# Attention operands laid out by the host: no transposes of q and k on the chip

## The chip, the cores and the metric

The kernel runs on one core of a Trainium2 chip. The metric is the device time of one execution in microseconds; lower is better. Three runs of the kernel before gave a median of 639.01 us (638.66 to 640.62).

## The reference

Three computations follow one another. All are float32 except the weights of the last, which arrive as 64-bit words.

```python
# attention, batch 2, 8 heads, 576 positions, head size 64
scores = q @ k.T / 8, masked; heads 0-3: 0 <= i-j < 32; heads 4-7: 0 <= i-j < 128 and (i-j) % 4 == 0
attn = softmax(scores);  x = (attn @ v), tokens 1152 x 512
# mixture: 4 experts, every token goes through all of them
out = sum_e p[:, e] * (relu(x @ w1[e]) @ w2[e])      # 512 -> 1024 -> 512
# last block
h = out @ w_in;  g = h * sigmoid(1.702 h);  result = g @ w_out   # 512 -> 2048 -> 512
```

## The kernel before

**Three stages.** Attention and the first expert are woven into each other and take about the first 156 us; then come the other three experts (line 799 on for the first product, 903 to 905 for the second), then the last block. Every large product is made of three products of rounded operands: high by high, low by high, high by low (`wh`, `wl`, `xh`, `xl`).

**Attention.** Heads are taken in pairs. Pairs 0 and 1 are "plain" (window 32), pairs 2 and 3 "dilated" (stride 4). The sequence of each batch is cut into a big and a small piece, so there are 16 parts, numbered 0 to 15 in the order of line 497: four big parts of batch 0 (pairs 2, 3, 0, 1), eight small ones, four big ones of batch 1. A big part has two groups, a small one has one; groups are numbered 0 to 23. A dilated part works by residue r of the position modulo 4, since a position sees only its own residue.

**Steps of a part or group.** `L` loads q and k of a part with tokens on partitions (`load_qk`, lines 213 and 217): rows of one position, 256 bytes a run for plain pairs and 1 KB for dilated ones. `T` transposes q or k on PE into PSUM (line 267; four transposes, two for a small plain part). `t` copies the transposed block to SBUF (line 270 on; `a` on ACT, `v` on DVE). `K` loads v (lines 232, 239, 243). `S` makes the scores of one group, or of two at once with their products alternating (line 324). `Q` masks them and takes the row minimum on DVE (line 332). `A` is the exponential with its row sum on ACT (line 337). `N` normalizes, on POOL (`p`) or DVE (`v`) (lines 358 to 360). `U` transposes the probabilities on PE (line 368), `c` copies them to SBUF, `V` multiplies by v (line 394), `C` and `R` store the result as high and low part `xh`, `xl`.

**The order** is written out by hand in `SCRIPT` (lines 22 to 58). Each word is emitted in that order, and every engine works through its own share of the words in that order; there is no other scheduler. Fillers from the first expert stand in the list: `W` loads a weight tile (line 144), `H` and `O` split it into high and low on ACT and on POOL or DVE (lines 159, 167), `G` and `F` are pieces of its first product (line 524), `2` of its second (lines 558 to 560), `h` and `l` the steps between. `P n` issues n "spin" products on constants (line 443). All loads are issued by SP from one queue, in list order.

**Dilated groups before.** `T` puts residues 0 and 2 of a head on partitions 0 to 63 and residues 1 and 3 on 64 to 127. Group x of a big dilated part takes the two residues of parity x for both heads (lines 294 to 301); its four score products all read one half of the partitions. In a small part the two halves are used in turn within each tile.

**Weights.** `w_load` (line 135) cuts a 128-row weight tile out of the full matrix. For the last block `w64_tasks` (line 703) loads 64-bit words in pieces of 512 KB, converts them and stores them to DRAM for later.

Of the kernel before, what the change touches and what calls it, by code (L numbers as in the profile page):

```python
# [27 lines left out]
G 0 1 h, R 3, N 6 v, T 5 k, T 5 q, U 6, L 7, W 1 1, K 3, c 5 v, O 0 0 p 0, t 4 k a, Q 7, A 7, c 6 a, H 1 0 0,
t 5 k a, t 4 q v, L 8, K 4, K 5, L 9, N 7 p, t 5 q v, V 5, C 5 v, S 8, G 0 1 l, S 9, T 6 q, U 7, T 7 k, F 0 7 8,
H 1 0 1, Q 8, R 5, O 1 0 v 2, L 10, W 2 0, K 6, D, A 8, K 7, O 1 0 p 1, N 8 p, G 0 2 h, G 1 1 l, T 6 k, T 7 q, U 8,  # L30
c 7 a, Q 9, t 6 q v, A 9, t 6 k v, K 8, W 3 0, L 11, t 7 q a, H 0 1 0, t 7 k a, c 8 v, N 9 v, V 7, S 10, F 1 0 1,
G 1 1 h, T 8 k, F 0 6 7, T 8 q, F 0 0 1, U 9, F 0 2 3, Q 10, C 7 a, A 10, H 0 1 1, R 7, O 1 0 v 0, F 0 3 6, F 1 6 7,
F 0 1 2, N 10 v, H 1 1 0, h 0, t 8 q v, c 9 v, O 0 1 v 0, t 8 k a, V 8, S 11, C 8 v, S 12, F 1 7 8, V 9, F 1 3 4,
F 1 2 3, T 9 q, Q 11, Q 12, A 12, A 11, l 0, O 0 1 v 1, F 1 5 6, R 8, F 1 4 5, O 1 0 p 3, F 2 1 6, T 10 q, U 10,
N 12 v, 2 0 0, F 2 0 1, F 1 1 2, O 0 1 v 2, c 10 a, K 9, L 12, L 13, K 10, N 11 p, U 11, T 9 k, t 9 q v, t 10 q v,
H 1 1 1, h 1, t 9 k a, C 9 a, F 2 6 8, c 11 v, O 0 1 v 3, T 10 k, U 12, t 10 k a, V 10, V 11, h 2, R 9, l 1, S 13,
c 12 v, H 2 0 0, S 14, C 11 a, V 12, l 2, R 11, O 2 0 p 0, Q 13, Q 14, H 3 0 0, C 12 a, T 11 q, 2 0 1, F 3 7 8,
2 1 0, 2 0 2, F 3 6 7, T 11 k, F 3 5 6, F 3 1 2, F 3 2 5, 2 0 3, F 3 0 1, 2 1 1, H 2 0 1, A 14, C 10 a, t 11 q v,
R 12, O 1 1 p 1, O 1 1 v 0, O 2 0 p 1, O 2 0 p 2, A 13, K 11, W 3 1, W 2 1, L 14, K 12, N 14 v, O 1 1 p 2, O 2 0 p 3,
R 10, h 3, t 11 k a, N 13 v, l 3, U 14, U 13, c 14 a, c 13 v, H 3 0 1, F 4 2 8, 2 1 2, 2 1 3, F 4 0 1, F 4 1 2, S 15,  # L40
V 14, h 4, V 13, C 14 a, H 3 1 0, H 2 1 0, H 2 1 1, R 14, C 13 v, R 13, O 3 0 p 1, O 1 1 v 3, O 3 0 p 2, O 2 1 p 2,
O 2 1 p 3, Q 15, 2 2 0, H 3 1 1, B 15 v, X 15, Y 15, F 5 0 2, 2 2 1, 2 3 0, F 5 2 5, F 5 5 8, 2 3 1, 2 2 2, T 12 k,
2 3 2, 2 2 3, O 3 0 p 3, l 4, N 15 v, t 12 k a, h 5, K 13, O 2 1 v 1, l 5, O 3 1 p 2, O 3 0 p 0, L 15, U 15, F 6 4 6,
F 6 2 4, F 6 6 8, 2 3 3, T 12 q, F 6 0 2, w, t 12 q v, c 15 a, V 15, h 6, S 16 17, l 6, Q 17, Q 16, C 15 a, B 16 v,
# [8 lines left out]
F 12 5 6, 2 9 3, F 12 3 4, c 20 v, t 15 k v, c 21 v, S 22, Q 22, S 23, Q 23, V 21, F 12 4 5, A 23, B 22 p, X 22,
h 12, Y 22, l 12, F 13 0 8, F 14 1 2, F 14 2 4, F 14 0 1, C 21 a, R 21, 2 11 0, N 23 v, N 22 v, h 13, 2 10 1, U 22,
2 10 2, 2 11 1, 2 10 3, 2 11 2, F 14 4 5, F 14 5 7, F 15 5 6, 2 11 3, F 14 7 8, 2 12 0, F 15 4 5, F 15 6 8, l 13,
c 22 v, F 15 3 4, U 23, h 14, 2 13 0, c 23 a, V 23, 2 12 1, C 23 v, 2 12 2, 2 12 3, 2 13 1, F 15 0 3, 2 13 2, h 15,
l 14, R 23, 2 13 3, l 15
# [4 lines left out]
def fused_kernel(ctx: ExitStack, tc: tile.TileContext, q, k, v, dp, w1, w2, w_in, w_out, out):  # L62
# [18 lines left out]
    B, H, S, D = q.shape  # L81
    NT, DM = out.shape
    E, _, FF1 = w1.shape
    FF2 = w_in.shape[1]
# [3 lines left out]
    NPAIR = H // 2  # L88
    J = S // 4
# [45 lines left out]
    def w_load(s, which):  # L135
        e, fp = divmod(s, F1 // 2)
        fs = slice(fp * 2 * P, (fp + 1) * 2 * P)
        if which == 0:
            t = stg.tile([P, KT, 2 * P], F32, tag="stg", name=f"st1_{s}")
            src = w1[e][:, fs].rearrange("(k p) f -> p k f", p=P) if e < E else late[s - 4 * E, 0]  # L140
        else:
            t = stg.tile([P, 2, DM], F32, tag="stg", name=f"st2_{s}")
            src = w2[e][fs, :].rearrange("(t p) d -> p t d", p=P) if e < E else late[s - 4 * E, 1]
        nc.sync.dma_start(out=t, in_=src)
        wst[s, which] = t
# [45 lines left out]
    raw = {}  # L191
# [15 lines left out]
    def load_qk(b, pr, kind):
        j0, j1 = t_part(b, pr, kind)
        for nm, src in (("q", q), ("k", k)):
            if plain(pr):  # L210
                t = ap_.tile([96, (j1 - j0) // 24, 2, D], F32, tag="raw", bufs=8, name=f"raw{nm}{b}{pr}{kind}")
                for h in range(2):
                    nc.sync.dma_start(out=t[:, :, h, :], in_=src[b, 2 * pr + h, 4 * j0:4 * j1, :].rearrange(
                        "(i s) d -> s i d", s=96))
            else:
                t = ap_.tile([j1 - j0, 2, 4, D], F32, tag="raw", bufs=8, name=f"raw{nm}{b}{pr}{kind}")
                nc.sync.dma_start(
                    out=t, in_=src[b, 2 * pr:2 * pr + 2, 4 * j0:4 * j1, :].rearrange("h (j r) d -> j h r d", r=4))
            raw[nm, b, pr, kind] = t

    def blocks_of(b, kind):
        j0, j1 = PARTS[b, kind]
        return range(j0 // 16, j1 // 16)

    def load_v(b, pr, kind):

        if plain(pr):
            bl = blocks_of(b, kind)
            t = ap_.tile([96, 6, 2, D], F32, tag="v", bufs=6, name=f"v{b}{pr}{kind}")
            i0 = bl[0]  # L230
            if i0 == 0:
                nc.sync.dma_start(out=t[:, 0, :, :], in_=v[b, 2 * pr:2 * pr + 2, 0:96, :].rearrange("h s d -> s h d"))
                i0 = 1
            n = bl[-1] + 1 - i0
            for h in range(2):
                head = v[b, 2 * pr + h]
                windows = bass.AP(tensor=head.tensor, offset=head.offset + (64 * i0 - 32) * D,
                                  ap=[[D, 96], [64 * D, n], [1, D]])
                nc.sync.dma_start(out=t[:, i0 - bl[0]:i0 - bl[0] + n, h, :], in_=windows)
        else:  # L240
            k0, k1 = {(0, "big"): (0, 96), (0, "small"): (64, 144), (1, "small"): (0, 64), (1, "big"): (16, 144)}[b, kind]
            t = ap_.tile([k1 - k0, 2, 4, D], F32, tag="v", bufs=6, name=f"v{b}{pr}{kind}")
            nc.sync.dma_start(
                out=t, in_=v[b, 2 * pr:2 * pr + 2, 4 * k0:4 * k1, :].rearrange("h (j r) d -> j h r d", r=4))
        vt[b, pr, kind] = t
# [913 lines left out]
```

## Time and profile before

| | before |
|---|---|
| median of 3 runs | 639.01 us (638.66 to 640.62) |
| span of the profiled execution, first to last instruction | 635.1 us |
| PE, DVE, ACT, POOL busy | 629.3, 483.7, 281.5, 355.1 us |
| DMA, all queues | 63.84 MB in 51497 packets |

The page gives no time of the profiled execution beside its span; the median of the runs lies 3.9 us above it. Busy time of PE is modelled, so 99% does not mean that PE is at its peak: idle time of PE, and who ended it, has to be read from the waits and the chain.

### The profile page before, as it was taken

The numbers are of one execution on the slowest core, as the hardware profiler recorded it, in microseconds if no ns is written. First come the engines' busy times: TensorE is split into PE (matmuls) and PEld (weight loads), VectorE is DVE, ScalarE is ACT, GpSimd is POOL, SyncE is SP. The second block draws the span as 40 slices with busy tenths as digits, with TensorE's granted clock in tenths as the row PEclk, the third lists the DMA queues.
The fourth block names the chain that finished last, engine by engine and source line by source line (L and its number), as shares of the span: only waits on it lengthen the run. The fifth ranks groups of instructions, "written<-read, shape, count | busy, mean of one in ns | idle before, by whom it ended". The sixth has DMA issues, their size and how long they took to land.

```text
span 635.1 us, 11563 instructions
## 1 busy us (share of the span) xinstructions
PE 629.3 (99%) x4313; PEld 585.3 (92%) x4314; DVE 483.7 (76%) x1025; ACT 281.5 (44%) x621; POOL 355.1 (56%) x334
## 2 busy tenths in 40 slices
PE   9999999999999999999999999999999999999998
PEld 6799999999999999999999999989898998998996
DVE  4885555296888878878889889999987757657655
ACT  6774342135534534534533534436735444344321
POOL 5334110366597697697687686579336653553310
PEclk9999999999999999999999999999999999999999
DMA  9966340101364365355365355221201212100003
GB/s 208 198 173 161 68 143 2 38 1 47 120 172 160 102 195 174 102 170 160 101 186 179 106 167 164 67 100 40 94 2 68 66 34 67 34 0 1 2 1 150
DMA packets 51497, 63.84 MB, mean 101 GB/s; under 512 B 20620, under 2 KB 33264, under 8 KB 51440
## 3 DMA queue, kind: packets, MB, share of 16 engines
q1 hardware_dynamic: 51440, 63.10, 34.8%
q8 instruction: 34, 0.56, 0.4%
q14 instruction: 23, 0.19, 0.1%
HBM read 52.32 MB, written 10.77 MB: 99 GB/s over the span
## 4 chain that ended last, share of the span: by engine, by line
PE 94%; DVE 3%; ACT 2%; issue 1%; DVEq 0%; ACTq 0%
PE gd L799 9%; PE gc L799 9%; PE ga L799 9%; PE g L524 8%; PE q L903 8%; PE q L905 8%; PE q L904 8%; PE q L933 5%; PE q L931 5%; PE q L932 5%; PE gb L799 5%; PE pa L558 3%; PE pa L560 3%; PE pa L559 3%; PE spin L443 1%
## 5 line engine op out<-in xcount | busy, mean ns | idle before, releaser
L903 PE MATMUL q<-h,w2h 128*128 128x320 f32 (+1 forms) x288 | 97.4, 338 | 0.1
L905 PE MATMUL q<-h,w2h 128*128 128x320 f32 (+1 forms) x288 | 97.2, 337 | 0.0
L904 PE MATMUL q<-h,w2l 128*128 128x320 f32 (+1 forms) x288 | 97.2, 337 | 0.0
L846 DVE TENSOR_TENSOR h<-cc,h 128x256 fp32r<-128x256 f32 (+1 forms) x80 | 74.1, 926 | 20.0 <-ACT h L836 12.5
L742 POOL TENSOR_TENSOR m<-m,sd 128x512 int32<-128x512 int32 x32 | 49.1, 1535 | 62.9 <-ACT h L836 37.2
L913 DVE TENSOR_TENSOR acc<-q,acc 128x512 f32<-128x512 f32 (+1 forms) x132 | 70.1, 547 | 9.2 <-PE q L905 7.8
L836 ACT ACTIVATE h<-cc 128x256 fp32r<-128x256 f32 (+3 forms) x48 | 32.9, 686 | 98.9 <-DVE cc L833 98.6
L679 POOL TENSOR_TENSOR wsl<-ss,wsh 128x512 fp32r<-128x512 f32 x39 | 59.2, 1525 | 31.0 <-ACT wsh L678 20.6
L821 POOL TENSOR_TENSOR cc<-s,u 128x256 f32<-128x256 f32 (+1 forms) x38 | 33.2, 873 | 59.9 <-DVE s L818 59.9
L905 PEld LDWEIGHTS q<-h,w2h 128*128 128x128 f32 x288 | 54.1, 188 | 4.4
L903 PEld LDWEIGHTS q<-h,w2h 128*128 128x128 f32 x288 | 54.1, 188 | 4.2 <-DVE acc L913 0.3
L904 PEld LDWEIGHTS q<-h,w2l 128*128 128x128 f32 x288 | 54.1, 188 | 3.9
L690 POOL TENSOR_TENSOR w2l<-st,w2h 128x512 fp32r<-128x512 f32 x37 | 53.9, 1469 | 5.5 <-ACT w2h L689 5.2
L933 PE MATMUL q<-w2h,h 128*128 128x512 f32 (+1 forms) x146 | 56.9, 390 | 0.0
L931 PE MATMUL q<-w2h,h 128*128 128x512 f32 (+1 forms) x146 | 56.7, 388 | 0.0
L932 PE MATMUL q<-w2l,h 128*128 128x512 f32 (+1 forms) x146 | 56.6, 387 | 0.0
L940 DVE SCALAR_TENSOR_TENSOR acc<-q,acc 128x512 f32<-128x512 f32 (+1 forms) x64 | 42.5, 677 | 11.7 <-PE q L933 11.3
L675 POOL TENSOR_TENSOR wal<-st,wah 128x512 fp32r<-128x512 f32 (+1 forms) x38 | 47.1, 1246 | 2.3 <-ACT wah L674 2.3
L799 PE MATMUL ga<-xh,wal 128*128 128x256 f32 (+1 forms) x160 | 47.3, 296 | 0.0
L799 PE MATMUL ga<-xl,wah 128*128 128x256 f32 (+1 forms) x160 | 47.3, 295 | 0.0
L799 PE MATMUL ga<-xh,wah 128*128 128x256 f32 (+1 forms) x160 | 47.2, 295 | 0.0
L833 DVE SCALAR_TENSOR_TENSOR cc<-cc,pb 128x256 f32<-128x256 f32 (+3 forms) x48 | 42.7, 890 | 1.0
(483 smaller groups left out, 1783.2 us busy)
## 6 DMA issues: line engine op xcount, KB each, us to landing
st<-in_moe_w_dram SPq DMA_DIRECT2D x32, 512.0 KB, 5.0
sd<-in_moe_w_in_dram SPq DMA_DIRECT2D x16, 512.0 KB, 4.2
sd<-in_moe_w_out_dram SPq DMA_DIRECT2D x16, 512.0 KB, 4.0
w<-m SPq DMA_DIRECT2D x32, 256.0 KB, 4.5
st<-w SPq DMA_DIRECT2D x16, 512.0 KB, 3.4
out_dram<-acc SPq DMA_DIRECT2D x8, 256.0 KB, 2.0
pb<-pd SPq DMA_DIRECT2D x3, 320.0 KB, 3.4
pb<-pd SPq DMA_DIRECT2D x3, 256.0 KB, 3.2
```

The lines of the kernel that those rows point to most:

```text
L524: nc.tensor.matmul(pt[:, :C], w[:, kt, fs], xx[:, kt, c * C:(c + 1) * C], start=first and y == 0, stop=not todo and y == len(products[x]) - 1)
L679: fns.append(lambda x=x, dst=dst: engine(f"p.{s}.{x}").tensor_tensor(out=sl[:, dst], in0=sums[:, dst], in1=sh[:, dst].bitcast(F32), op=ALU ...
L690: fns.append(lambda o=o: engine(f"q.{s}.{2 * o + 1}").tensor_tensor(out=lo[:, o], in0=t[:, o], in1=hi[:, o].bitcast(F32), op=ALU.subtract))
L799: nc.tensor.matmul(bank_[:, :n], wz[:, y, m, :], xz, start=start and m == 0 and z == 0, stop=m == 1 and z == 2, skip_group_check=not start)
L846: nc.vector.tensor_tensor(out=hl[:, sub], in0=cc[:, sub], in1=hh[:, sub].bitcast(F32), op=ALU.subtract)
L903: nc.tensor.matmul(pt, wh[:, o, cols], hi, start=first, stop=False, skip_group_check=both)
L904: nc.tensor.matmul(pt, wl[:, o, cols], hi, start=False, stop=False, skip_group_check=both)
L905: nc.tensor.matmul(pt, wh[:, o, cols], lo, start=False, stop=last, skip_group_check=both)
L913: nc.vector.tensor_tensor(out=dst[:, on], in0=pt[:, on], in1=src[:, on], op=ALU.add)
L931: nc.tensor.matmul(pt, hi, wh[:, o, cols], start=o == 0, stop=False)
L932: nc.tensor.matmul(pt, hi, wl[:, o, cols], start=False, stop=False)
L933: nc.tensor.matmul(pt, lo, wh[:, o, cols], start=False, stop=o == 1)
```

## The change

The host rearranges the inputs before launch (no arithmetic): for each of the 16 parts, q and k of a head pair are stored as 128 rows (head, d) by tokens, the queries first and then all keys that the part needs, halo included; for dilated parts the columns go by residue. v is stored by key blocks as the products read it. The weights are stored as the 128-row tiles that the kernel loads, each row contiguous.

On the chip `load_qk` becomes one DMA into a tile `qkT` of up to 896 columns (9 buffers), and `load_v` one DMA. The steps `T` and `t` are gone from the list, with their PSUM banks; 16 parts had 112 transposes and 32 copies. `S 0` and `S 1` become one step `S 0 1` (before, they stood apart, with `T 1` between them). All other words of the list keep their order; the spins `P` stay. A dilated group now holds one head and all four residues (big part), or both heads in the two halves of each tile (small part).

```diff
-P 6, P 1, L 0, M, L 1, L 2, W 0 0, L 3, T 0 q, K 0, P 1, T 0 k, t 0 q a, P 1, P 2, t 0 k v, S 0, Q 0, T 1 q, T 1 k,
-t 1 q v, t 1 k v, A 0, S 1, Q 1, W 0 1, L 4, ...
+P 6, P 1, L 0, M, L 1, L 2, W 0 0, L 3, K 0, P 1, P 1, P 2, S 0 1, Q 0, A 0, Q 1, W 0 1, L 4, L 5, K 1, K 2, L 6,
...
+    def load_qk(b, pr, kind, rows=None):
+        off, w, _, _ = QK_AT[b, pr, kind]
+        if (b, pr, kind) not in qkT:
+            qkT[b, pr, kind] = ap_.tile([P, 896], F32, tag="qkT", bufs=9, name=f"qkT{b}{pr}{kind}")
+        src = qk[off:off + P * w].rearrange("(p w) -> p w", w=w)
+        a, z = (0, P) if rows is None else (rows * D, rows * D + D)
+        nc.sync.dma_start(out=qkT[b, pr, kind][a:z, :w], in_=src[a:z])
...
     def load_v(b, pr, kind):
+        off, rows, w = V_AT[b, pr, kind]
+        t = ap_.tile([P, 768], F32, tag="v", bufs=6, name=f"v{b}{pr}{kind}")
+        nc.sync.dma_start(out=t[:rows, :w], in_=v[off:off + rows * w].rearrange("(p w) -> p w", w=w))
...
-    def do_T(b, pr, kind, bank, nm):
...
             elif kind == "big":
                 self.rows = 96
-                q0, k0, self.n, m = (0, 0, 96, mA) if b == 0 else (48, 16, P, mB)
-                for t in range(2):
-                    r = 2 * t + x
-                    for h in range(2):
-                        base = (2 * h + t) * J
-                        tiles.append(([(0, 96, x, base + q0, base + k0)], m, [(0, 96, 96 * r, h, r)]))
+                self.n, m = (96, mA) if b == 0 else (P, mB)
+                for r in range(4):
+                    tiles.append(([(0, 96, x, r * nq, 4 * nq + r * nk)], m, [(0, 96, 96 * r, x, r)]))
...
     def w_load(s, which):
-            src = w1[e][:, fs].rearrange("(k p) f -> p k f", p=P) if e < E else late[s - 4 * E, 0]
+        src = (w1, w2)[which][s].rearrange("p (a b) -> p a b", a=t.shape[1]) if s < 4 * E else late[s - 4 * E, which]
...
+            src = (w_in, w_out)[which][fp].bitcast(U32)[:, 2 * o * DM:2 * (o + 1) * DM]
+            nc.sync.dma_start(out=t.rearrange("p d w -> p (d w)"), in_=src)
```

## Rows read from the trace of the kernel before

**Rows 1.** The page: busy time of the engines, and the DMA packets by size.

```profile
PE 629.3 (99%) x4313; PEld 585.3 (92%) x4314; DVE 483.7 (76%) x1025; ACT 281.5 (44%) x621; POOL 355.1 (56%) x334
...
DMA packets 51497, 63.84 MB, mean 101 GB/s; under 512 B 20620, under 2 KB 33264, under 8 KB 51440
```

**Rows 2.** Stretches: us; busy PE, PEld, DVE, ACT, POOL; granted clock; DMA share; GB/s.

```profile
0.00:7.00 7.00, 6.18 (x27) 3.46 (x27) 0.56 (x1) 1.77 (x2) 5.07 (x25) 1.00 0.69 178
7.00:17.00 10.00, 9.05 (x118) 7.21 (x117) 8.30 (x60) 8.97 (x42) 4.63 (x7) 1.00 1.17 226
17.00:30.00 13.00, 12.78 (x167) 9.95 (x168) 10.84 (x55) 10.13 (x46) 4.18 (x7) 1.00 1.07 210
30.00:48.00 18.00, 18.00 (x235) 16.54 (x232) 15.65 (x73) 13.96 (x54) 5.69 (x8) 1.00 0.65 166
48.00:115.00 67.00, 67.00 (x563) 63.66 (x562) 36.47 (x136) 22.38 (x63) 14.26 (x19) 1.00 0.35 88
180.00:190.00 10.00, 10.00 (x71) 10.00 (x70) 7.73 (x15) 4.85 (x9) 8.78 (x8) 1.00 0.69 201
```

**Rows 3.** Waits of PE, 0 to 155 us: total, times, longest.

```profile
PE ppt03big L368 <- DVE pT03big L274: 0.6, 1, 0.6
PE ppt02big L368 <- POOL prob02big L360: 0.5, 1, 0.5
```

**Rows 4.** The chain that ended last, 0 to 20 us: start, length, what.

```profile
0.76 3.14 PE spin L443 x7
...
5.61 0.68 PE spin L443 x3
...
6.36 0.90 PE s02big L324 x8
...
7.40 0.25 DVE prob02big L332
...
8.20 0.47 DVE qT L274
8.67 0.46 DVE kT L274
...
9.34 1.54 ACT prob02big L337 x8
10.88 0.37 ACT kT L272
11.25 0.52 ACT wh L159
```

**Rows 5.** The same chain: transposes of q and k, first and last.

```profile
17.63 0.37 PE pTk02small L267 x4
...
92.98 0.33 PE pTq11big L267 x4
```

**Rows 6.** Timeline of PE, behind a block of transposes: start, length.

```profile
59.63 0.42 PE L558 MATMUL pa<-h,wh 128*128 128x384 f32 x1
59.89 0.34 PE L559 MATMUL pa<-h,wl 128*128 128x384 f32 x1
```

**Rows 7.** Timeline of PE, and of POOL, around group 8 (part 4).

```profile
24.55 0.77 PE L324 MATMUL s02small<-kT,qT 64*64 64x80 f32 x16
28.77 0.61 PE L368 MATMUL ppt02small<-ident,prob02small 128*80 128x128 f32 x4
...
27.84 0.72 POOL L360 TENSOR_TENSOR prob02small<-prob02small,st02small 128x320 f32<-128x320 f32 x1 [2.01 <-DVE st03small L332]
```

**Rows 8.** The chain at the border to the next stage.

```profile
155.68 0.18 PE pa L560
155.86 0.71 PE ga L799 x6
```

**Rows 9.** DMA issues: number, KB each, median us to landing.

```profile
st<-in_moe_w_dram SPq DMA_DIRECT2D x32, 512.0 KB, 5.0
...
rawq02big<-in_q_dram SPq DMA_DIRECT2D x1, 192.0 KB, 2.6
```

More of the change, by code (lines that the diff above doesn't have):

```diff
@@ L28 @@
[L28 to L32, printed above, removed]
@@ L53 @@
[L53 to L57, printed above, removed]
+S, D, J, NPAIR = 576, 64, 144, 4
@@ new lines, with plain, blocks_of, spans @@
+KINDS = {(0, "big"): (0, 96), (0, "small"): (96, 144), (1, "small"): (0, 48), (1, "big"): (48, 144)}
+PARTS = [(b, pr, kind) for b, kind in KINDS for pr in range(NPAIR)]
+def plain(pr):
+    return pr < NPAIR // 2
+def blocks_of(b, kind):
+    j0, j1 = KINDS[b, kind]
+    return range(j0 // 16, j1 // 16)
+def spans(b, kind):
+    return {(0, "big"): ((0, 96), (0, 96)), (0, "small"): ((80, 144), (64, 144)), (1, "small"): ((0, 64), (0, 64)),
+            (1, "big"): ((48, 144), (16, 144))}[b, kind]
@@ new lines, in tokens, with windows, places @@
+def tokens(b, pr, kind):
+    if plain(pr):
+        bl = blocks_of(b, kind)
+        return [list(range(a, 64 * bl[-1] + 64)) for a in (64 * bl[0], max(0, 64 * bl[0] - 32))]
+    return [[4 * j + r for r in range(4) for j in range(*span)] for span in spans(b, kind)]
+def windows(b, pr, kind):
+    if plain(pr):
+        return [list(range(a, a + 96)) for a in (max(0, 64 * i - 32) for i in blocks_of(b, kind))]
+    return [[4 * j + r for j in range(*spans(b, kind)[1])] for r in range(4)]
+def places():
+    qk, v, at, vat = {}, {}, 0, 0
+    for part in PARTS:
+        nq, nk = (len(x) for x in tokens(*part))
+        rows = windows(*part)
+        per = 1 if plain(part[1]) else 4
+        qk[part] = (at, nq + nk, nq // per, nk // per)
+        v[part] = (vat, len(rows[0]), len(rows) * 2 * D)
+        at += P * (nq + nk)
+        vat += len(rows[0]) * len(rows) * 2 * D
+    return qk, v
@@ L58, with fused_kernel @@
+R 23, 2 13 3, l 15
 """
 @with_exitstack
-def fused_kernel(ctx: ExitStack, tc: tile.TileContext, q, k, v, dp, w1, w2, w_in, w_out, out):
+def fused_kernel(ctx: ExitStack, tc: tile.TileContext, qk, v, dp, w1, w2, w_in, w_out, out):
     nc = tc.nc
-    B, H, S, D = q.shape
     NT, DM = out.shape
-    E, _, FF1 = w1.shape
-    FF2 = w_in.shape[1]
+    E = dp.shape[1] // (NT // P)
+    FF1, FF2 = w1.shape[0] // E * 2 * P, w_in.shape[0] * 2 * P
     C = 384
@@ L207, in load_qk @@
[L207 to L211, printed above, removed]
-                for h in range(2):
[L213 to L219, printed above, removed]
@@ L221, in blocks_of @@
-    def blocks_of(b, kind):
-        j0, j1 = PARTS[b, kind]
-        return range(j0 // 16, j1 // 16)
-    def load_v(b, pr, kind):
[L227 to L245, printed above, removed]
@@ L270, in keep @@
+    def load_v(b, pr, kind):
+        off, rows, w = V_AT[b, pr, kind]
+        t = ap_.tile([P, 768], F32, tag="v", bufs=6, name=f"v{b}{pr}{kind}")
+        nc.sync.dma_start(out=t[:rows, :w], in_=v[off:off + rows * w].rearrange("(p w) -> p w", w=w))
+        vt[b, pr, kind] = t[:rows, :w].rearrange("p (x h d) -> p x h d", h=2, d=D)
     def keep(eng, out, in_):
@@ L286, in __init__ @@
             tiles = []
+            _, _, nq, nk = QK_AT[b, pr, kind]
             if plain(pr):
@@ L290, in __init__ @@
                 for i in bl[3 * x:3 * x + 3]:
-                    k0 = max(0, 64 * i - 32)
-                    tiles.append(([(64 * h, 64, h, 64 * i, k0) for h in range(2)], mP if i else mP0,
+                    k0 = max(0, 64 * i - 32) - max(0, 64 * bl[0] - 32)
+                    tiles.append(([(64 * h, 64, h, 64 * (i - bl[0]), nq + k0) for h in range(2)], mP if i else mP0,
                                   [(64 * h, 64, 64 * (i - bl[0]), h, i - bl[0]) for h in range(2)]))
@@ L295, in __init__ @@
                 self.rows = 96
-                q0, k0, self.n, m = (0, 0, 96, mA) if b == 0 else (48, 16, P, mB)
-                for t in range(2):
-                    r = 2 * t + x
-                    for h in range(2):
-                        base = (2 * h + t) * J
-                        tiles.append(([(0, 96, x, base + q0, base + k0)], m, [(0, 96, 96 * r, h, r)]))
+                self.n, m = (96, mA) if b == 0 else (P, mB)
+                for r in range(4):
+                    tiles.append(([(0, 96, x, r * nq, 4 * nq + r * nk)], m, [(0, 96, 96 * r, x, r)]))
             else:
                 self.rows = P
-                q0, k0, self.n, m, o = (80, 64, 80, mP[:, 16:], 16) if b == 0 else (0, 0, 64, mP0[:, :64], 0)
-                for t in range(2):
-                    for h in range(2):
-                        base = (2 * h + t) * J
-                        tiles.append(([(64 * y, 64, y, base + q0, base + k0) for y in range(2)], m,
-                                      [(64 * y + o, 48, 48 * (2 * t + y), h, 2 * t + y) for y in range(2)]))
+                self.n, m, o = (80, mP[:, 16:], 16) if b == 0 else (64, mP0[:, :64], 0)
+                for r in range(4):
+                    tiles.append(([(64 * h, 64, h, r * nq, 4 * nq + r * nk) for h in range(2)], m,
+                                  [(64 * h + o, 48, 48 * r, h, r) for h in range(2)]))
             self.tiles = tiles
@@ L317, in products @@
                 g.sps = ps.tile([P, 4, P], F32, tag="ps", name=f"s{g.nm}")
-                qt, kt_ = (qkT[nm, g.b, g.pr] for nm in "qk")
-                return [(g.sps[p0:p0 + w, i, :g.n], qt[x * D:(x + 1) * D, qc:qc + w], kt_[x * D:(x + 1) * D, kc:kc + g.n])
+                t = qkT[g.b, g.pr, g.kind]
+                return [(g.sps[p0:p0 + w, i, :g.n], t[x * D:(x + 1) * D, qc:qc + w], t[x * D:(x + 1) * D, kc:kc + g.n])
                         for i, (some, _, _) in enumerate(g.tiles) for p0, w, x, qc, kc in some]
@@ L400, in values, with attention @@
         return lambda eng: keep(eng, dh, src), rest
-    def attention(parts, bank):
+    def attention(parts):
         flat = []
@@ L414, in attention @@
         steps = {
-            "T": lambda j, nm: do_T(*parts[j], bank, nm),
-            "t": lambda j, nm, eng: keep(eng, *turned.pop((nm, *parts[j]))),
-            "L": lambda j: load_qk(*parts[j]),
+            "L": lambda j, rows=None: load_qk(*parts[j], rows),
             "K": lambda j: load_v(*parts[j]),
@@ L500, in fused_kernel @@
     parts += [(1, pr, "big") for pr in ORDER]
-    steps = attention(parts, bank)
+    steps = attention(parts)
     hbuf = {}
@@ L712, in load @@
             t = st_["t"] = late["sd"].tile([P, DM, 2], U32, tag="sd", name=f"sd{u}")
-            if which == 0:
-                src = w_in.bitcast(U32)[2 * o * P:(2 * o + 2) * P, fp * 4 * P:(fp + 1) * 4 * P].rearrange(
-                    "(k p) w -> p k w", p=P)
-                dst = t.rearrange("p (k f) w -> p k (f w)", k=2)
-            else:
-                f = 2 * fp + o
-                src = w_out.bitcast(U32)[f * P:(f + 1) * P, :]
-                dst = t.rearrange("p d w -> p (d w)")
-            nc.sync.dma_start(out=dst, in_=src)
+            src = (w_in, w_out)[which][fp].bitcast(U32)[:, 2 * o * DM:2 * (o + 1) * DM]
+            nc.sync.dma_start(out=t.rearrange("p d w -> p (d w)"), in_=src)
         def a():
@@ L961, in fused_kernel @@
         "Z": p_turn,
-        "D": lambda: nc.sync.dma_start(out=pw, in_=dp.rearrange("(t p) e -> p t e", p=P)),
+        "D": lambda: nc.sync.dma_start(out=pw, in_=dp.rearrange("p (t e) -> p t e", e=E)),
     })
@@ L1130, in fused_kernel, with _laid_out, cat, pair @@
     assert not queue and at64[0] == len(units64) + 1 and not rounds and not deferred
-_INS = ["q", "k", "v", "moe_domain_probs", "moe_w1", "moe_w2", "moe2_w_in", "moe2_w_out"]
 _OUTS = [((1152, 512), "float32")]
+def _laid_out(q, k, v, moe_domain_probs, moe_w1, moe_w2, moe2_w_in, moe2_w_out):
+    import numpy as np
+    def cat(parts):
+        return np.concatenate([np.ascontiguousarray(x).reshape(-1) for x in parts])
+    def pair(x, b, pr, cols):
+        return x[b, 2 * pr:2 * pr + 2][:, cols].transpose(0, 2, 1).reshape(P, -1)
+    qk_, v_ = [], []
+    for b, pr, kind in PARTS:
+        qs, ks = tokens(b, pr, kind)
+        qk_ += [np.concatenate([pair(q, b, pr, qs), pair(k, b, pr, ks)], axis=1)]
+        rows = np.array(windows(b, pr, kind))
+        v_ += [v[b, 2 * pr:2 * pr + 2][:, rows].transpose(2, 1, 0, 3)]
+    def first(w):
+        d, f = w.shape
+        return w.reshape(d // P, P, f // (2 * P), 2 * P).transpose(2, 1, 0, 3).reshape(f // (2 * P), P, -1)
+    def second(w):
+        f, d = w.shape
+        return w.reshape(f // (2 * P), 2, P, d).transpose(0, 2, 1, 3).reshape(f // (2 * P), P, -1)
+    n, e = moe_domain_probs.shape
+    return {
+        "qk": cat(qk_),
+        "v": cat(v_),
+        "dp": moe_domain_probs.reshape(n // P, P, e).transpose(1, 0, 2).reshape(P, -1),
+        "w1": np.concatenate([first(w) for w in moe_w1]),
+        "w2": np.concatenate([second(w) for w in moe_w2]),
+        "w_in": first(moe2_w_in),
+        "w_out": second(moe2_w_out),
+    }
 def kernel(**inputs):
@@ L1145 @@
     arrays, args = {}, []
-    for name in _INS:
-        a = _np.ascontiguousarray(inputs[name])
+    for name, a in _laid_out(**inputs).items():
+        a = _np.ascontiguousarray(a)
         if a.dtype == _np.float64:
```

91 lines of the change are left out of this document (30 added, 61 removed).

## The prediction

> **What bounds the kernel now.** I began with the busy line of the page: PE is busy 629.3 of 635.1 us, DVE 76%, ACT 44%, POOL 56% [rows 1]. PE is then the first suspect, but its ends are modelled, so the next view was the table by stretch. In the attention stage PE fills 9.05 of the 10 us from 7 to 17, 12.78 of 13 to 30 us, and all of the two stretches after; DVE is at 83%, 83%, 87% and 54% in the same four, ACT at 90%, 78%, 78% and 33%, and DMA at a share above 1 from 7 to 30 us and 0.65 and 0.35 later [rows 2]. The waits of PE up to 155 us that are waits for another engine's work are two, of 0.6 and 0.5 us, both before 17.1 us [rows 3]. So there are two regimes. Up to 17 us the chain of waits goes through ACT and DVE; it runs through spins, two transposes, two copies, exponentials and weight copies [rows 4]. From 17.6 us on the chain is PE without a break, and the transposes stand on it. The first `L799` product of the next stage, at 155.86 us [rows 8], comes straight after PE's own last product, so whatever PE saves before that point moves the whole rest.
>
> **The change, part by part.** The sum is made against the profiled span of 635.1 us. The median of the unprofiled runs is 639.0, 3.9 us above it; I let these 3.9 us stand and subtract the gain from the median.
>
> *Start, to 17.6 us.* The first scores wait for two transposes and two copies and begin at 6.36 [rows 4]. Without them PE has 11 spins in a row (six, one, one, one, two). Seven take 3.14 us, so 0.43 to 0.45 each, until about 5.4 us. The data are there earlier: the 192 KB of q of this part land 2.6 us after issue [rows 9]; one DMA of 384 KB at the 226 GB/s of rows 2 needs 0.9 us more, so it lands near 4.2 us. Scores start 0.95 us sooner. `S 0` and `S 1` become one interleaved step, so the second group's scores no longer come behind the transposes of part 1, nor its masking behind two DVE copies (0.47 and 0.46 us [rows 4]). The first masking ends at 7.40 + 0.25, 1.3 us after the first score [rows 4], and releases ACT's first exponential, so now at about 6.7; two groups at 1.54 us each end at 9.8 instead of 10.88. Then the kT copy of 0.37 us on ACT's chain goes [rows 4], and the weight copy begins at 9.8 instead of 11.25. Term: 1.5 us. From there ACT works back to back to the last piece before PE takes over, so this carries through. Bounds: 0.95 (only the earlier score) to 2.4 (ACT waits nowhere and the other early copies count too).
>
> *17.6 to 30 us.* The chain holds 24 blocks of transposes between 17.63 and 93.3 us, of 0.17 to 0.39 us each; the first and the last are shown [rows 5]. They sum to 7.1 us, 8 blocks a stretch: 2.7 us up to 30, 2.0 up to 48, 2.4 up to 115. In this first stretch not all of it can be had. The scores of part 4 start at 24.55, POOL finishes normalizing them at 27.84 + 0.72 = 28.56, and PE turns them at 28.77 [rows 7]. Four blocks (1.3 us) lie between, inside a latency of 4.2 us of DVE, ACT and POOL: without them PE only waits. Of the other 1.4 us I take half, 0.7, since DVE is at 83% and sets when probabilities are ready; bounds 0 and 2.7.
>
> *30 to 48 us.* 2.0 us of blocks; PE has no wait here, but DVE is busy 15.65 of 18 us [rows 2]. DVE sheds copies as well (the list gives it 17 of the 32 copies of qT and kT), but its chain from masking to normalizing stays. I take two thirds, 1.3 us; bounds 0 and 2.4.
>
> *48 to 115 us.* 2.4 us of blocks. The fp32r product behind a block pays too: 0.26 us from 59.63 to 59.89, against 0.17 for its neighbours (0.18 for the last product before 155.86) [rows 6, 8]. With 8 blocks at 0.09 this makes 3.1 us. DVE at 54% and ACT at 33% follow easily. I take 2.7; bounds 2.0 and 3.1.
>
> *After 115 us.* Nothing changes on PE. Weights come in 4 KB rows instead of 1 KB or 2 KB, but the DMA share is 0.69 even in a busy stretch such as 180 to 190 us [rows 2]; 0, bounds minus 0.5 and 0.5. The cover is the load issued two units ahead; were it gone, a 512 KB transfer would show, 5.0 us at landing [rows 9].
>
> *Loads.* q and k become one DMA a part (9 buffers of 896 columns), v one. The SP queue loses some 60 issues; it holds no new wait that bites, since the tenth load waits only for the first scores. q and k grow by about 0.5 MB from halo keys. What the tighter order asks for: by the first values of part 3, right behind the turn at 28.77 [rows 7] and about 2.1 us sooner now, 5.72 MB must have landed (eight q and k loads 2.64, four weight tiles 2.10, four v loads 0.98). From 2.4 us on that is 231 GB/s. Rows 2 show 226 and 210 where the queue was saturated with short pieces, and 166 at a share of 0.65 or 201 at 0.69 elsewhere, 255 to 291 at a full share by proportion. I take about 260: hidden.
>
> The page counts 20620 of 51497 packets under 512 bytes [rows 1]. By the Trainium skill ("DMA: Bandwidth & Descriptors", Specifications) transfers under 512 bytes miss the line rate; by that rule the new layout only gains. It lowers the chance of the load rival below and leaves the sum.
>
> *Scores by head.* Before, a dilated group held one parity of r and both heads; now one head and all four r. Number, shape and half of the array are unchanged: the old group x also read only one half of the rows. 0; if the two halves stopped running side by side, four paired steps would cost some 0.9 us more each, 3.6 us.
>
> Sum: 1.5 + 0.7 + 1.3 + 2.7 = 6.2 us. Span 628.9, time **632.8 us**.
>
> **Rivals.**
>
> *All of it is released.* If DVE, ACT and POOL speed up with PE, since they shed 32 copies, the gain is 1.5 + 7.1 + some 0.9 behind blocks = 9.5 us: 629.5. For it: waits are nearly absent [rows 3]. Against it: the 0.2 us between POOL's end and the turn at 28.77 [rows 7].
>
> *The clock falls.* The first seven spins take 0.45 us each, the three at 5.61 us 0.23 [rows 4]: the two levels, 1.2 and 2.4 GHz, although the granted clock of the table reads 1.00 [rows 2]. Some 4.9 us of spins stood before the change of level. Between 7 and 17 us PE loses its transposes and has nothing to put there, so it stands idle for 2 us after the first four groups of scores. If the clock falls there, the dense stretch starts at half speed: 4.9 us at half is 2.4 us lost, and about 1 us of turns and values on the chain doubles. Gain 2.8: 636.2. The Trainium skill ("TensorE: Matmul & The Clock Gate", What's actually happening) says that idleness throttles the array; its Part 4 says that transposes do not count as activity in the same way, by which little cover is taken away. No row of before shows a fall after 5.6 us.
>
> *Loads become the bound.* At 215 GB/s, the mean of the two saturated rows, 5.72 MB land at 29.0 us, 1.8 us after they are wanted. Gain 4.4: 634.6.
>
> *Slower.* The same place, but rows of 2 to 3.5 KB move no faster than the first 7 us, 178 GB/s [rows 2]. The values of part 3 would wait until 34.5 us, 5.2 later than before; the later gains give back 4.0: 640.2. It decides below 185 GB/s. Against it: the 178 includes the ramp, and every full stretch moved more.
>
> *Not what it says.* The halves stop running side by side: 636.4.
>
> **How the numbers follow.** Forecast (630.6 to 634.5) 0.54; all released 0.19; loads 0.10; clock 0.10; halves 0.02; slower 0.03; nothing comes through although PE does less 0.02. Under 0.3% (1.9 us) a change can't be told from none. The clock and halves cases end close above that bound, so some of their weight goes to "same". Faster 0.91, same 0.05, slower 0.04. Range: 629.0 to 636.0 leaves out about 0.08 below and 0.11 above.
>
> **What would show it.** Right: first scores near 5.4 us; weight copy on ACT near 9.8; the turn of part 4 near 26.6; the first `L799` product near 149.7, with the same distance to the end as before; no packets of 256 bytes. PE's waits before 50 us should grow to 2 or 3 us in sum, on POOL and DVE; without them, the first rival. A wait on a DMA near 27 us is the load rival. fp32r products spaced 0.3 us or more after 15 us are the clock. Wrong altogether: a first `L799` product after 154 us, or a gain there that is lost again later.

## Result and profile after

The changed kernel takes 631.46 us (median of five executions, 631.23 to 633.74), the kernel before beside it 638.66. The ratio is 0.9903, 95% interval 0.9876 to 0.9931: faster by 1.0%. The forecast was 632.8 us, range 629.0 to 636.0. The profiled execution has a span of 629.7 us, against 635.1.

The page of the changed kernel: busy time of the engines, and the DMA packets by size.

```profile
PE 619.1 (98%) x4201; PEld 575.3 (91%) x4202; DVE 475.1 (75%) x1008; ACT 276.3 (44%) x606; POOL 355.3 (56%) x334
...
DMA packets 23174, 64.33 MB, mean 102 GB/s; under 512 B 2764, under 2 KB 4336, under 8 KB 23120
```

Against [rows 1] TensorE has 112 instructions fewer, the 112 transposes, and DMA has 28,000 packets fewer, of which 18,000 were under 512 bytes.

The stretches of the changed kernel, columns as in [rows 2].

```profile
0.00:7.00 7.00, 6.24 (x39) 2.92 (x41) 0.14 (x1) 1.28 (x1) 5.04 (x25) 1.00 0.64 225
7.00:17.00 10.00, 6.50 (x83) 4.67 (x80) 6.93 (x56) 9.44 (x45) 5.64 (x8) 1.00 1.04 318
17.00:30.00 13.00, 10.95 (x157) 8.78 (x157) 10.30 (x61) 9.45 (x42) 3.15 (x5) 1.00 0.88 228
30.00:48.00 18.00, 17.58 (x204) 16.10 (x203) 14.55 (x61) 12.99 (x49) 5.82 (x8) 1.00 0.54 179
48.00:115.00 67.00, 66.96 (x543) 63.41 (x543) 33.82 (x129) 19.25 (x55) 18.58 (x21) 1.00 0.24 79
```

In the second stretch TensorE fell from 9.05 to 6.50 busy us, in the third from 12.78 to 10.95: what it no longer has to do there it mostly spends waiting. In the last it is still full, so there less work means an earlier end. Loads ran at 318 GB/s from 7 to 17 us, where the forecast took 260 and rows 2 show 226: no load came late.

The waits of PE in the changed kernel, 0 to 150 us (total, times, longest), those on another engine's work.

```profile
PE ppt02big L344 <- POOL prob02big L336: 2.4, 1, 2.4
PE ppt02small L344 <- POOL prob02small L336: 1.4, 1, 1.4
PE ppt03big L344 <- POOL prob03big L336: 0.8, 1, 0.8
PE ppt00big L344 <- ACT prob01big L313: 0.5, 1, 0.5
PE ppt00small L344 <- POOL prob00small L336: 0.4, 1, 0.4
```

In [rows 3] these were two waits of 0.6 and 0.5 us. Now there are five, 5.5 us in sum, 5.0 of them on the normalization on POOL.

The chain that ended last in the changed kernel, 0 to 17 us: start, length, what.

```profile
0.76 4.85 PE spin L417 x11
5.62 1.15 PE s02big L300 x16
...
6.86 0.25 DVE prob02big L308
...
7.16 1.55 ACT prob02big L313 x8
...
9.27 0.82 POOL prob02big L336
...
10.14 0.54 PE ppt02big L344 x4
...
13.21 1.44 ACT prob03big L313 x8
...
15.19 0.83 POOL prob03big L336
...
16.07 0.55 PE ppt03big L344 x4
```

No transpose and no copy stands ahead of the scores any more. The first masking began at 7.40 [rows 4] and begins at 6.86, only 0.54 us sooner, because the eleven spins, and the scores behind them until 6.11 us, ran at the lower clock level: 4.85 us for eleven spins is 0.44 each, the long spacing of rows 4.

Timelines of PE, ACT and POOL of the changed kernel: the first weight copy, the normalization and the turn of the first small part, and two later marks.

```profile
10.04 0.61 ACT L197 ACTIVATE wh<-st 128x512 fp32r<-128x512 f32 x1
...
26.23 0.72 POOL L336 TENSOR_TENSOR prob02small<-prob02small,st02small 128x320 f32<-128x320 f32 x1 [1.45 <-DVE st03small L308]
...
27.01 0.63 PE L344 MATMUL ppt02small<-ident,prob02small 128*80 128x128 f32 x4 [1.42 <-POOL prob02small L336]
...
46.45 0.49 PE L344 MATMUL ppt10small<-ident,prob10small 128*96 128x128 f32 x3
```

The border to the next stage in the chain of the changed kernel.

```profile
150.53 0.18 PE pa L528
150.71 0.71 PE ga L760 x6
```

The first product of the next stage (old line `L799`) moved from 155.86 [rows 8] to 150.71, by 5.15 us; from there to the end it is 479.0 us, before 479.2.

### The profile page after: what moved, and what is told of

It is laid out like the page before. It is cut to its first block, busy times and chain, and to the rows that moved or that the text cites. A ratio compares the mean times of both kernels' runs of the same rounds, so it can differ in the third digit from the quotient of the medians.

```text
span 629.7 us, 11219 instructions
## 1 busy us (share of the span) xinstructions
PE 619.1 (98%) x4201; PEld 575.3 (91%) x4202; DVE 475.1 (75%) x1008; ACT 276.3 (44%) x606; POOL 355.3 (56%) x334
## 2 busy tenths in 40 slices
DMA packets 23174, 64.33 MB, mean 102 GB/s; under 512 B 2764, under 2 KB 4336, under 8 KB 23120
## 4 chain that ended last, share of the span: by engine, by line
PE 92%; DVE 4%; ACT 2%; issue 1%; POOL 0%; POOLq 0%; ACTq 0%; DVEq 0%
PE gd L760 10%; PE gc L760 9%; PE ga L760 9%; PE q L864 8%; PE q L866 8%; PE q L865 8%; PE g L492 7%; PE q L894 5%; PE q L892 5%; PE q L893 5%; PE gb L760 5%; PE pa L526 3%; PE pa L528 3%; PE pa L527 3%; PE spin L417 1%
```

## Experiments

Each kernel ran beside the kernel before on the same chip, and the ratio is against that. Three marks are compared where a trace is used: the second turn of group 3 (U 3, the last row of the chain above, 17.09 before), the turn U 8 (28.77 [rows 7]) and the first `ga` product. The clock of an execution is its mean granted clock.

**e1, e2: transposes back, then copies too.** The new loads and layouts stay; the old order of steps returns with its transposes. They turn the identity matrix, a constant, and nothing reads the result.

```diff
+            nc.tensor.transpose(pt[:, x * n:(x + 1) * n], ident[:n, :], ident[:n, :n])
+        keep(eng, scr[eng][:, :src.shape[1]], src)      # e2 alone: the 32 copies
-S 0 1
+S 0, ..., S 1
```

> The changed kernel with the old list, less its copies: 112 transposes of a constant stand in their old places on PE, S 0 and S 1 apart, and nothing reads the result. Loads and layout stay new. Theory (the gain is PE's path): the span rises from 629.7 to between 633.5 and 635.0, the first L799 product of before (150.7 us in the changed kernel) to 154.5 to 156.0, and by 2.0 to 2.6 us of it after 50 us. Rival (the gain is the loads): span within 1 us of 629.7. Rival (the gain is the relief of DVE and ACT by 32 copies): span 630 to 631.5.

> As the kernel with transposes of a constant, and each is copied from PSUM to a spare tile by the engine that did it before (17 on DVE, 15 on ACT); nothing reads the copy. Theory (PE's path, with the copies counting only up to 48 us): 0.3 to 1.2 us over the kernel with transposes alone, and within 1 us of the kernel before (635.1). Rival (copies): 3 us or more over the kernel with transposes alone. Rival (loads): within 1.5 us of 629.7.

Measured: e1 635.87 us, ratio 0.9953 (0.9929 to 0.9978), span 634.8; e2 636.73 us, ratio 0.9968 (0.9949 to 0.9986), span 634.7.

PE timeline of e1: U 3 and the first product of the next stage.

```profile
17.42 0.54 PE L369 MATMUL ppt03big<-ident,prob03big 96*96 96x96 f32 x4 [0.59 <-POOL prob03big L361]
...
155.74 0.28 PE L792 MATMUL ga<-xh,wah 128*128 128x256 f32 x1
```

From U 3 to that product e1 needs 138.3 us, e2 138.6, the kernel before 138.6 (17.09 to 155.70 in the same view), the changed one 134.5 (16.07 to 150.55). So 112 transposes bring back 3.8 of the 4.1 us, the copies 0.3 at most. In the times the two intervals overlap, and the copies are worth somewhere from nothing to 0.9 us. Among executions with a clock of 0.999 or 1.0 the medians are 635.66 us (e1), 636.60 (e2) and 636.92 (the kernel before, beside them), against 631.34 for the changed kernel. PE's path is the main cause. The rest of the distance to the kernel before, 0.3 to 0.5%, isn't on this path, since the spans are alike (634.7 and 635.1); it comes up again below.

**e3: weights laid out as before**, all else as in the changed kernel.

```diff
-            src = (w1, w2)[which][s].rearrange("p (a b) -> p a b", a=t.shape[1])
+            src = w1[e][:, fs].rearrange("(k p) f -> p k f", p=P)
```

> The changed kernel with w1, w2, w_in and w_out as the inputs have them, cut into tiles by the DMAs as before (1 KB and 2 KB pieces); q, k and v stay in the new layout. Theory: no difference, within 0.6 us of 629.7, since weights are issued ahead of use and the DMA share is under 0.7 after 30 us. Rival (loads are part of the gain): 1.5 to 3 us more, with a wait of ACT or PE on a DMA in the first 40 us.

Measured: 631.21 us, ratio 0.9889 (0.9864 to 0.9914), span 629.5, waits of PE the same to a tenth of a microsecond, although the packets rise from 23,174 to 33,414. The weights' layout is worth nothing here.

**e4: normalization on VectorE** for the four groups whose turn waits on POOL.

```diff
-N 0 p, ... N 3 p, ... N 8 p, ... N 11 p
+N 0 v, ... N 3 v, ... N 8 v, ... N 11 v
```

> The changed kernel with four normalizations (groups 0, 3, 8, 11) on DVE instead of POOL; PE waited 2.4, 0.8, 1.4 and 0.4 us for these. Theory (between 7 and 40 us the latency from scores to turned probabilities holds the gain back): each of the four waits falls by 0.2 to 0.4 us and the span by 0.3 to 1.5 us. Rival (DVE itself is the bound there, busy 79% to 81%): the waits only move, and the span stays or rises by up to 1 us.

Measured: 633.50 us (633.25 to 634.00), ratio 0.9926 (0.9900 to 0.9951). In sum the waits became no smaller, they moved, as the rival said: 2.1 on ACT's exponentials, 1.6, 0.9 and 0.7 on DVE, 6.0 us with two short ones. POOL was only the last link of a latency that masks, exponentials and sums on DVE and ACT fill. And the clock fell. The stretches of e4:

```profile
7.00:18.00 11.00, 6.62 (x89) 4.89 (x89) 8.70 (x59) 9.49 (x48) 4.38 (x6) 1.00 1.05 316
18.00:25.00 7.00, 6.28 (x43) 4.95 (x40) 4.62 (x20) 3.04 (x15) 0.67 (x1) 0.53 1.05 239
```

From 18 to 25 us the granted clock is 0.53, that is 1.2 GHz for nearly all of it, behind 11 us with 4.4 us of idle TensorE. All six executions show it (0.994 or 0.995).

**e5, e6, e7: spins added to, or taken from, the idle time.** e5 is the changed kernel with nine spins for one ahead of U 0; e6 is e4 with these and four more ahead of U 3; e7 is the changed kernel without the four spins that stand between 7 and 13 us.

```diff
-P 1, U 0
+P 9, U 0                 # e5, e6 (e6 also: P 4, U 3)
-P 1, U 0 ... P 2, U 1 ... P 1, N 3 p
+U 0 ... U 1 ... N 3 p    # e7
```

> The changed kernel with nine spins instead of one before the first turn U 0, where PE stood idle from 7.5 to 10.1 us. In two of five executions of the changed kernel the mean granted clock was 0.994 and the span 2.2 us longer. Theory (that idle stretch lets the clock fall in some executions): all executions have clock 1.000 and the span stays at 629.4 to 629.9, so the slower two disappear; the fast ones gain nothing. Rival (the fall has another cause, or is chance): the same share of executions at 0.994. Rival (spins are in the way): span 0.3 us or more above 629.9 in all.

> The kernel with groups 0, 3, 8, 11 normalized on DVE, which showed half the clock from 18.4 to 25.2 us, with nine spins before U 0 and four before U 3. Theory (its 2.2 us over the changed kernel were the clock's, and latency holds the gain back): clock 1.000 and span 628.6 to 629.6. Rival (DVE is the bound in 7 to 40 us): clock 1.000 and span 630 to 631, with waits of PE on DVE in place of those on POOL. Rival (the clock does not depend on these idle stretches): clock 0.995, span 631.5 to 632.5.

> The changed kernel without its last three spin steps (one, two and one spins between 7 and 13 us). Theory (PE's activity between 7 and 17 us holds the clock, and the transposes had been part of what was left in it): the half clock shows in most or all executions, mean 0.994 or less, span 631.5 to 633.5. Rival (spins there do nothing): clock 1.000 in three of five or more, span 629.4 to 629.9.

Measured: e5 631.44 us (630.29 to 631.76), ratio 0.9886 (0.9859 to 0.9912); e6 631.66 (630.90 to 633.02), 0.9895 (0.9868 to 0.9921); e7 631.84 (630.96 to 634.76), 0.9910 (0.9876 to 0.9943). e6 against e4 is the clean pair: spins do no work and release nothing, and yet 633.5 becomes 631.7; five of six executions of e6 now have a clock of 0.999 or 1.0, none of e4 had. e7 splits: two executions at clock 1.0 take 631.0, two at 0.992 take 631.8, two at 0.989 take 634.6. e5 lost the executions at 633.6 that the changed kernel has, but its median is that kernel's. The five of e6 at 0.999 and 1.0 have a median of 631.52 us, against 631.34 for the changed kernel: the normalization on VectorE gains nothing with the clock up either.

The expectation of e5, a clock of 1.0 in all, failed: two of six fell, the traced one among them. Stretches of e5, and below them of e7, whose traced execution did not fall:

```profile
7.00:18.00 11.00, 8.81 (x99) 5.92 (x98) 7.82 (x59) 10.68 (x53) 6.04 (x8) 1.00 1.04 326
18.00:21.00 3.00, 3.00 (x20) 2.28 (x19) 2.79 (x8) 0.19 (x1) 0.00 (x0) 0.50 1.05 280
```

```profile
7.00:17.00 10.00, 5.71 (x82) 4.28 (x80) 7.16 (x57) 9.72 (x48) 6.05 (x8) 1.00 1.04 312
```

So spins in the idle time made falls rarer here (e4 6 of 6, e6 1 of 6), but the idle time ahead doesn't decide the single execution.

**e8: scores first.** The spins that stand ahead of `S 0 1` behind the first seven go; twelve stand in the gap ahead of U 0.

```diff
-K 0, P 1, P 1, P 2, S 0 1, ... A 2, P 1, U 0
+K 0, S 0 1, ... A 2, P 12, U 0
```

> The changed kernel with four of its first eleven spins moved behind the first four groups of scores (twelve spins before U 0). q and k of the first part had landed at 4.0 us, but PE reached S 0 1 at 5.55 behind its spins. Theory (the start is set by these spins, and what it gains runs through ACT to PE): first scores at 4.1 to 4.3, the weight copy on ACT 0.7 to 1.3 us sooner than 10.04, span 628.4 to 629.3 at clock 1.000. Rival (loads are next: the copy waits for the first weight tile, or scores for the second part): start gains 0.5 us or less, span 629.3 to 629.8. Rival (the clock rises later, or falls): span above 630.

Measured: 629.95 us (629.83 to 630.20), ratio 0.9866 (0.9838 to 0.9894), span 628.1, clock 1.0 in all five. The start of its chain:

```profile
0.72 3.22 DMA qkT02big<-in_qk_dram
3.94 0.04 issue
3.98 1.14 PE s02big L301 x16
5.12 0.90 PE s03big L301 x16
6.02 2.73 PE spin L418 x12
8.74 0.26 PE ppt02big L345 x3
```

The data are there at 3.94 (the forecast: 4.2), and in the changed kernel the scores still stood behind spins for 1.6 us. In this pair of traces the 1.6 us pass through undiminished: U 3 16.07 to 14.48, U 8 27.01 to 25.41, first `ga` product 150.55 to 148.96, span 629.7 to 628.1. But the rise of the clock differs too, 6.11 us in the one and 4.47 in the other. At like rises the order alone is worth less: the first exp stands at 6.35 in e5 (rise 4.34) and 5.57 in e8 (4.47), 0.8 us; at 7.08 in e3 (5.92) and 5.88 in e12 below (5.91), which begins as e8 does, 1.2 us. What lies between that and the 1.4 us by which the medians of executions at 0.999 and 1.0 differ (631.34 to 629.95) isn't shown. In e9 and e10 below, with the first exp at 5.38 and 5.39, ACT then waits 0.3 and 0.5 us for the first weight tile, so the load is the next limit of the start.

**e9: fill the wait of U 8.** e8 with ready work ahead of it.

```diff
-U 8, c 7 a, ... V 7, S 10, F 1 0 1
+c 7 a, V 7, S 10, U 8, ... F 1 0 1
```

> The early-scores kernel (e8, 629.95 us, span 628.1) with the copy c 7, the values V 7 and the scores S 10 put ahead of the turn U 8, so that TensorE has 1.6 us of ready work in its 1.4 us wait for the small part's norm on GpSimd. Theory (behind 30 us TensorE sets the end, so a wait filled early is taken off the end one for one): V 7 can start about 24.4 us, when ACT has copied its turn; U 8 comes 0.3 to 0.6 us later than in e8 but 1.5 us of work lies ahead of it: the first product of the first expert at 148.0 to 148.3 us (e8: 148.96), span 627.2, median 629.0 (ratio about 0.985). Rival (another engine bounds 25 to 36 us: the later turns then wait as much longer for VectorE, ACT or GpSimd): first product at 148.8 to 149.2, median 629.7 to 630.2.

Measured: 630.70 us (630.00 to 630.73), ratio 0.9888 (0.9872 to 0.9904), first `ga` product at 149.10. The rival was right on the product; the median lies 0.5 us above its range. The turns in the PE timeline of e9:

```profile
25.64 0.63 PE L345 MATMUL ppt02small<-ident,prob02small 128*80 128x128 f32 x4
...
27.96 0.61 PE L345 MATMUL ppt03small<-ident,prob03small 128*80 128x128 f32 x4 [0.98 <-DVE st12small L309]
```

U 8 waits no more, but U 9 now waits 0.98 us, with DVE's row named as the last. That I took a filled wait for a gained one was the error: behind one latency stood the next.

**e10: e8 without the spins in the gap; e11: the changed kernel again.**

```diff
-A 2, P 12, U 0
+A 2, U 0
```

> The early-scores kernel (e8) without the twelve spins ahead of U 0: TensorE then idles about 2.7 us between 6.0 and 8.7 us. Start theory (the gain of e8 comes from the scores that no longer stand behind four spins): where the clock stays up the time is that of e8, 629.8 to 630.3 us, span 628.1. Clock theory (a TensorE idle for that long in its first 10 us at full clock falls to half in part of the executions): 2 to 4 of 6 executions show a granted clock below 0.997 and 631.5 to 632.5 us, as in the kernels with 5.7 to 6.5 us of TensorE work between 7 and 17 us, while e8 (8.6 us) showed none in 5. If no execution falls, the spins in the gap are worth nothing and the falls of the changed kernel hang on something else.

> The changed kernel as it is, again, for more executions beside e8's kind and e10: 631.2 to 631.6 us where the granted clock is 1.0 and 633.6 to 633.8 us where it is 0.994, the latter in 1 to 4 of 6; a time at clock 1.0 outside 630.5 to 632.0 would say that the chip, not the clock, spreads these kernels.

Measured: e10 631.95 us (631.10 to 632.04), ratio 0.9909 (0.9893 to 0.9925); all five executions have a clock of 0.994 to 0.997. e11 631.29 (631.11 to 633.62), ratio 0.9908 (0.9889 to 0.9927), 631.33 and 631.34 at clock 1.0 and 633.62 at 0.994, as expected. The stretches of e10, and below them of e8:

```profile
7.00:17.00 10.00, 6.68 (x88) 5.01 (x89) 6.88 (x49) 9.27 (x45) 6.05 (x8) 1.00 1.04 305
17.00:21.00 4.00, 3.77 (x23) 3.12 (x24) 3.59 (x16) 1.02 (x6) 0.00 (x0) 0.57 1.05 328
```

```profile
7.00:17.00 10.00, 8.62 (x97) 5.75 (x95) 7.08 (x50) 9.61 (x49) 6.05 (x8) 1.00 1.04 334
17.00:21.00 4.00, 3.83 (x49) 3.10 (x51) 3.26 (x14) 1.34 (x7) 0.00 (x0) 1.00 1.05 284
```

Without the twelve spins e8's whole gain is gone, and its clock with it. From 17 to 21 us e10 gets 23 products done where e8 gets 49. The Trainium skill ("TensorE: Matmul & The Clock Gate", What's actually happening) says that the throttled state is the default and that activity releases it; e10 against e8 agrees: twelve products without any use make the difference between five falls in five executions and none in five.

**e12: the small part's own row earlier.** e8 with `S 8`, its masks and its exps one step forward.

```diff
-H 1 0 0, ... N 7 p, V 5, C 5 v, S 8, ... Q 8, ... A 8
+N 7 p, S 8, Q 8, V 5, C 5 v, A 8, H 1 0 0
```

> The early-scores kernel (e8, 629.95 us, span 628.1, U 8 at 25.41 behind a wait of 1.40, first expert product at 148.96) with the scores S 8 of the first small pair, their masks and their exps one step earlier: S 8 and Q 8 ahead of the values V 5, A 8 ahead of the weight copy H 1 0 0 on ACT. No work is added or left out. Theory (what ends the wait at U 8 is the pair's own row: scores, masks, exp on ACT, norm on GpSimd; e9 filled the wait with other work and only moved it to U 9): scores at about 20.4 instead of 21.2 us, first exp at about 21.7 instead of 22.6, U 8 at 24.4 to 24.7, U 9 no later than in e8, first expert product at 148.0 to 148.4, median 629.0 to 629.4. Rival (V 5 and the copies pushed back by 0.7 us hold the products of g and U 9 as much longer, as in e9): first product at 148.8 to 149.2, median 629.8 to 630.2. Second rival (two reports of the same kernel differ by the clock alone): a median over 630.5 with a granted clock below 0.999 in most executions.

Measured: 632.33 us (631.69 to 633.57), ratio 0.9906 (0.9882 to 0.9931), a clock of 0.994 to 0.997 in all six. POOL's timeline in e12, and PE's at U 8:

```profile
24.35 0.72 POOL L206 TENSOR_TENSOR wl<-st,wh 128x256 fp32r<-128x256 f32 x1 [1.48 <-ACT wh L198]
25.82 0.72 POOL L337 TENSOR_TENSOR prob02small<-prob02small,st02small 128x320 f32<-128x320 f32 x1 [0.74 <-DVE st03small L309]
...
26.59 1.08 PE L345 MATMUL ppt02small<-ident,prob02small 128*80 128x128 f32 x4 [2.21 <-POOL prob02small L337]
```

The exps did come earlier (22.27 against 22.58 us), but the weight copy that I put behind them on ACT came later, and POOL, which has its low half (`O 1 0 p 1`) queued ahead of the normalization, waited for it until 24.35. U 8 came 1.2 us later than in e8, behind a wait of 2.21 us, and that turn took 1.08 us for 0.63: the clock had fallen at 26.4. e12 was my error in queue order; it shows once more what follows an idle TensorE.

**All executions by their clock.** Below 0.998: e4 6 of 6, e10 5 of 5, e12 6 of 6, e7 4 of 6, the changed kernel 6 of 11, e3 2 of 6, e5 2 of 6, e6 1 of 6, e8 and e9 none of 5. The kernel before: 28 of 56; these have a median of 639.88 us, the other 28 one of 637.10. e1 and e2, with nearly the same work on TensorE: 3 of 24, where the kernel before beside them on the same chip fell in 15 of 23.

## Why the prediction was right, step by step

The sum was 6.2 us; the profiled spans differ by 5.4.

| step | foretold | measured | from |
|---|---|---|---|
| start, to U 3 | 1.5 | 1.02 | 17.09 to 16.07 |
| 17.6 to 30 us, to U 8 | 0.7 | 0.74 | 28.77 to 27.01, less 1.02 |
| 30 to 48 us, to U 14 | 1.3 | 0.97 | 49.18 to 46.45, less 1.76 |
| 48 to 115 us | 2.7 | 2.42 | 5.15 at the border, less 2.73 |
| after | 0 | 0.25 | 635.1 less 629.7, less 5.15 |

*Start.* The mechanism was right, the size half again too large: ACT's first weight copy begins at 10.04 us, foretold 9.8. Some 0.2 of the missing 0.5 us is the sum itself: eleven spins from 0.76 us on, at the forecast's own 0.43 to 0.45 each, end at 5.5 to 5.7, not at 5.4, and in the trace at 5.62. By an estimate from the slope below about 0.26 is the clock's rise: its record in the trace shows the full level from 5.55 us in the execution before and from 6.11 in the one after. Over five kernels that begin alike (the changed one, e3, e4, e5, e6) the first exp follows that moment closely, 6.35 us at a rise of 4.34 (e5) to 7.16 at 6.11, or 0.46 us per us. The forecast had let the rise stay where it was. It also took the wait behind the spins as given, though its own figures had the data there 1.2 us before the scores; e8 shows that it was worth 0.8 to 1.2 us more at a like rise of the clock.

*17.6 to 48 us.* The argument that four blocks of transposes lie inside a latency that stays held: PE's wait at U 8 is 1.4 us, where 1.3 was expected to turn into waiting. In sum the waits before 50 us are 5.5 us, not 2 to 3, since the first gap, 2.4 us ahead of U 0, was priced only under the clock rival. The one behind U 8, ahead of `ppt00small` (0.4), is about what is missing in the third term.

*48 to 115 us.* No wait, as foretold. Behind U 13 start-to-start times give 2.1 us for the transposes, which leaves 0.3 for the products next to them. My 0.09 for each of eight blocks was too much: over all 24 blocks the start-to-start times sum to 6.4 us, the lengths in the chain to 7.1, so part of the switch was in the lengths already.

*Loads, scores by head, after 115 us.* Nothing, as costed, and so none of these rivals came: no wait on a DMA, `S 0 1` in 0.94 us where its scores ran mostly at the full clock (e7), the distance to the end within 0.2 us, and e3 the same without the new weights. The sign of no packets of 256 bytes can't be read off: 2,764 packets under 512 bytes are left, and the page doesn't tell them apart.

*The clock.* The forecast said that no row of before shows a fall, and gave the rival one chance in ten for the time of the median. It happened in part: 3 of 11 executions of the changed kernel fell to 0.994 and took 633.6 to 633.7, 2.3 us more than the 631.23 to 631.46 of those at 1.0. I had 3.4. Three more show 0.996 or 0.997 and take no longer than those at 1.0 (631.11 to 631.25). That is luck in the one that was traced (e11): its fall, at 11.0 to 14.4 us, cost 0.6 us, and a clock that had risen at 4.15 us instead of 6.11 had gained 0.9 before. TensorE wasn't waiting there, as its stretch shows; below it the chain of e11: first exp, the turns U 0 and U 1, U 3.

```profile
11.00:14.00 3.00, 2.85 (x20) 2.06 (x20) 1.31 (x9) 2.24 (x11) 1.80 (x3) 0.50 1.06 294
```

```profile
6.26 1.55 ACT prob02big L313 x8
...
9.24 0.54 PE ppt02big L344 x4
...
11.79 0.65 PE ppt02big L344 x4
...
15.81 0.55 PE ppt03big L344 x4
```

From U 0 to U 3 these are 6.57 us; in the changed kernel's first trace, and in e5, it is 5.93. Whether transposes count for the clock as other products do, as one sentence of the rival has it, no run here settles: e1 and e2 have them and seldom fall, the kernel before has them and often does.

*The 3.9 us between span and median*, which I let stand, were the part of the profile that I read too lightly. Of these, 1.8 us are a constant (635.1 us of span in executions that take 636.9). The rest is most likely the clock, though the three runs have none on record: a profile at 1.0 stood beside the median of a kernel that falls in half of its executions. So the forecast of 632.8 us came as near to 631.46 as it did partly by luck: it began 2.1 us too high and took 0.8 us too much off the span, and with the constant alone it would have been 630.7. Compared at clocks of 0.999 and 1.0 alone the change gains 5.8 us (637.10 to 631.34), over all executions 6.8 (638.16 to 631.34), so about 1 us of the gain is that the changed kernel loses less to the clock. Something that came with the layouts takes part: e1 and e2, with the new loads, the old work on TensorE and no scores that wait for a copy, fell in 3 of 24. Why the kernel before falls so often, with 9.05 us of work in its second stretch, stays open; no trace of such an execution was taken, and the one that I have shows no idle time to blame.

The best version is e8: 629.95 us, 1.5 us below the changed kernel, and none of its five executions fell.

## What to carry to other kernels

Taking work off a saturated engine pays in full only where that engine alone bounds; ask of each piece whether it stood inside another engine's latency, and count it there as new idle time. Then ask what that idle time does to the clock: here useless products in the gap were worth 2 us. And look at the clock of every execution, not at the profiled one's alone, before a difference between span and median is put down to noise.

## What the runs showed of the hardware

The moment at which the clock rises at the start differs between executions that issue the same spins, from 4.15 to 6.11 us in two traces of one kernel (e11 and the first of the changed kernel), and the first exp with it, from 6.26 to 7.16. A difference of some tenths of a microsecond between the spans of two traces can be that alone. The Trainium skill ("TensorE: Matmul & The Clock Gate", Part 1) says that the number of slow matmuls at the start varies from run to run of one kernel; these two traces agree.

A fall of the granted clock costs by where it lies, not by its mean. So in three traced executions with a mean of 0.997 and one fall each: at 11.0 us it cost 0.6 us (e11), at 17.4 us 1.1 (e10: 135.6 us from U 3 to the first `ga` product, 134.5 in e8), at 18.0 us 1.1 (e5: 135.5).

Loads of the first stage moved 318 GB/s over ten microseconds with the new rows, and 226 with the old ones [rows 2].
